# The softmax probabilities of a step kept in two tiles, one for each exp

## The chip, the core and the metric

The kernel runs on one core of one Trainium2 chip. A core has engines that run their own instruction streams in parallel and meet through semaphores: TensorE (PE: matmuls; its weight loads are shown as PEld), VectorE (DVE), ScalarE (ACT), GpSimd (POOL) and SyncE (SP, which here issues most DMAs). Matmul results land in PSUM, everything else on the chip lies in SBUF, and big tensors lie in DRAM.

The metric is the time of one execution on the device in microseconds (us); the median over several runs is compared.

## The reference, cut to what matters

A transformer block on 2048 tokens of width 448 with 16 heads of 28, modulated by a vector `c`:

```
mod = silu(c) @ w_mod                       # sa, ca, ga, sb, cb, gb
h = layernorm(x) * (1 + ca) + sa
q, k, v = split_heads(h @ wqkv)             # 16 heads of 28
p = softmax(q k^T / sqrt(28))
x = x + ga * ((p v) @ wo)
h = layernorm(x) * (1 + cb) + sb
x = x + gb * (gelu(layernorm(h) @ w1 + b1) @ w2 + b2)
```

The change lies in the attention: `p` and its product with `v`.

## The kernel before, in words

**Stages.** A first phase makes the modulation, the layer norm, Q, K and V, and some of the row maxima of the scores. The attention follows, and then the MLP. Float32 values are split into a high and a low part in several places, so that products are made as hi*hi + lo*hi + hi*lo.

**The attention loop** (`for u in range(NU)`, line 1140). A unit `u` is a group of four heads and a block of 512 queries: 4 x 4 = 16 units. A unit has 16 steps `kt`, one for each block of 128 keys, so there are 256 steps. A step does, in this order of issue:

- line 1152: takes the tile `pt` for the probabilities of the step: 128 keys x 4 heads x 512 queries.
- lines 1158 to 1168, for the two halves `hf` (heads 0 and 1, then heads 2 and 3): six scores matmuls into a PSUM tile of two banks (line 1163: three terms for each of two heads, the first with 29 rows, of which the last brings in the row maximum, the others with 28), and then one exp by ScalarE over the two banks into the half of `pt` (line 1168). Between them stand matmuls for row maxima of later units (`emit_max`, matmul line 466), each followed by a reduction on VectorE (line 471) that frees its PSUM tile. A step has three or four of them in turn while there are any left.
- line 1174: the product of probabilities and V of the step *before* (`av`, line 1133), so that TensorE has something to do while ScalarE makes the exps.
- tasks due in this step (line 1182): the end of earlier units, loads, in the last four units the output projection (`t_wo`), and in the end the preparation of the MLP.

Two PSUM tiles for scores (`s1`, `s0`) go in turn, so that the first half of a step waits for the first exp of the step before, and the second half for its second exp. When all maxima are done, a third one is opened (`third_tile`). Three PSUM tiles serve the maxima in this loop.

**What sets the order.** The program is written out in the order in which each engine issues it; no scheduler moves instructions. The tile layer only adds the waits: an instruction that reads or overwrites a tile waits for the semaphores of those that wrote or read it before. It knows the parts of a tile: of a tile `[128, 4, 512]` the two halves are kept apart when read, while a new tile in the same slot waits for all that used the old one. An instruction holds one wait; where it needs more, the others stand on event-semaphore instructions ahead of it in the same engine's stream.

**The slots.** `slot(tag, ...)` (line 77) gives a piece of SBUF by name, used by one tile after another. `c0`, `c1` and `d0` are 4 x 512 float32 on each partition, and are used through the whole kernel: for the modulation weights (`wm_ac`, line 164), the parts of `h` of odd token blocks (`hT`, line 283), as scratch for a Relu (`pair_diff`, line 477), for the probabilities (`ptags`, line 1138, in turn by `step % 3`), and in the end for parts of `w1` and `w2` (lines 1008 to 1094). `slot4` (line 83) hands out a four-part slot, for the tags in `halved` as two tiles with names `tag` and `tag + "h"`.

Of the kernel before, what the change touches and what calls it, by code (L numbers as in the profile page):

```python
# [13 lines left out]
F32 = mybir.dt.float32  # L14
F32R = mybir.dt.float32r
AF = mybir.ActivationFunctionType
# [6 lines left out]
D = 448  # L23
# [3 lines left out]
NC = 4  # L27
# [8 lines left out]
SCALE = float(DH) ** -0.5  # L36
# [3 lines left out]
def tile_adaln_block(ctx: ExitStack, tc: tile.TileContext, x, wqkv, wo, w1, b1, w2, b2, c, w_mod, out):  # L40
    nc = tc.nc
    pe, act, dve, pool, sp = nc.tensor, nc.scalar, nc.vector, nc.gpsimd, nc.sync
# [27 lines left out]
    def nm(t):  # L70
        uid[0] += 1
        return f"{t}_{uid[0]}"
# [4 lines left out]
    def slot(tag, shape, dt=F32R):  # L77
        return sb.tile(shape, dt, tag="slot_" + tag, name=nm("slot_" + tag), bufs=1)


    halved = ("a2", "a3", "b1")

    def slot4(tag, inner):
        if tag not in halved:
            t = slot(tag, [128, 4] + inner)
            return lambda k: t[:, k]
        t2 = [slot(tag + h, [128, 2] + inner) for h in ("", "h")]
        return lambda k: t2[k // 2][:, k % 2]

    def ps_s2():  # L90
# [4 lines left out]
    def ps_s():  # L95
        return ps_tile("pa", 2)
# [11 lines left out]
    def f(t):  # L108
        return t.bitcast(F32)
# [11 lines left out]
    sa_col, ca_col = cols[:, 0:NC], cols[:, NC:]  # L121


    d0 = slot("d0", [128, 4, 512], F32)
    sil_b = d0[:, 0, 0 : NC * 32].rearrange("p (k r) -> p k r", r=32)
    c_rows = d0[0:NC, 1, :128]
    sp.dma_start(c_rows[0:3], c[0, 0:384].rearrange("(k p) -> k p", p=128))
    acc = [sbt(f"acc{b}", [128, 4, D]) for b in range(NB)]

# [13 lines left out]
    def load_w(cs, dst):  # L143
        for k in range(3):
            sp.dma_start(dst(k), wqkv[128 * k : 128 * k + 128, cs])
        sp.dma_start(dst(3)[0:64], wqkv[384:D, cs])
        sp.dma_start(dst(3)[64:128], wqkv[384:D, cs])

    def load_mod(dst, k, c0, n):
        if k < 3:  # L150
            sp.dma_start(dst[:, : n * D], w_mod[128 * k : 128 * k + 128, c0 : c0 + n * D])
        else:
            for h in range(2):
                x0 = c0 + h * n * D // 2
                sp.dma_start(dst[64 * h : 64 * h + 64, : n * D // 2], w_mod[384:D, x0 : x0 + n * D // 2])


    def mod_part(k, j, n):
        if k < 3:
            return slice(0, 128), slice(j * D, (j + 1) * D)  # L160
        h, j = divmod(j, n // 2)
        return slice(64 * h, 64 * h + 64), slice(j * D, (j + 1) * D)

    wm_ac = [slot(f"c{i}", [128, 2, 2 * D], F32) for i in range(2)]
    for k in range(NC):
        load_mod(wm_ac[k // 2][:, k % 2, :], k, 0, 2)
    load_w(slice(0, 2 * D), lambda k: raw_qk[k // 2][:, k % 2, :])
    sp.dma_start(acc[1], xv[1])
    load_w(slice(2 * D, 3 * D), lambda k: raw_v[:, k, :])
# [126 lines left out]
    pm = ps_s()  # L296
# [11 lines left out]
    for k in range(NC):  # L308
        for j in range(2):
            rs_, cs = mod_part(k, j, 2)  # L310
            pe.matmul(
                pm[32 * j : 32 * j + 32, :D], sil_b[rs_, k, :], wm_ac[k // 2][rs_, k % 2, cs],
                start=(k == 0), stop=(k == NC - 1),
            )
    warm_up(2)
# [18 lines left out]
    v_sb = [sb.tile([128, 4, H, 32], F32, tag=f"slot_v{i}", name=f"v{i}", bufs=1) for i in range(4)]  # L334
# [15 lines left out]
    def by_head(t):  # L350
        return t.rearrange("(j r) n -> j r n", r=32)

    ones = d0[0:4, 0, 128:384]
    pool.memset(ones, 1.0)

    ones_d = dr.tile([4, S], F32, tag="ones", name="ones_d", bufs=1)
# [100 lines left out]
    px_no = [0]  # L457

    def max_mm(g, qt, i, j, k, ps=None):
        if (g, qt) not in mxp:  # L460
            mxp[(g, qt)] = sbt("mxp", [128, 4, 4, 4], bufs=6)
            if (g, qt) in paired:
                pool.memset(mxp[(g, qt)][:, :, :, 0:1], -3.0e38)
        m = (ps or ps_mx)()
        js = slice(32 * j, 32 * j + DH)
        pe.matmul(m, qh_sb[(g, qt)][js, i * 128 : (i + 1) * 128], k[js, :], start=True, stop=True)  # L466
        return m
# [6 lines left out]

    def pair_diff(g, qt, i, j):
        m = max_mm(g, qt, i, j, k_diff[0])
        r = d0[:, 1 + px_no[0] % 3]
        px_no[0] += 1
        act.activation(r, m, AF.Relu)  # L479

        def rest(ps):
            m = max_mm(g, qt, i, j, kh_sb[(g, 0)], ps)
            dve.tensor_tensor_reduce(
                out=r, in0=m, in1=r, scale=1.0, scalar=-3.0e38, op0=ALU.add, op1=ALU.max,
                accum_out=mxp[(g, qt)][:, i, j, 1:2],
            )

        return rest
# [121 lines left out]
    def finish_max(g, qt):  # L610
        while left[(g, qt)] > 0:
            emit_max(1)
# [47 lines left out]
    def load_q(u):  # L660
        g, qt = divmod(u, NB)
        qst[u] = load_parts(f"b{u % 2}", 0, g, slice(qt * 512, (qt + 1) * 512))
# [21 lines left out]
    for n, i in (  # L684
# [7 lines left out]
        p, ts = firsts[n]  # L692
# [3 lines left out]
    for b in range(NB):  # L696
# [12 lines left out]
        for n, (tb, kind, g) in enumerate(tasks):  # L709
# [9 lines left out]
            k = n - (6, 4, 4, 4)[b]  # L719
# [17 lines left out]
            if more:  # L737
                k = n - (6, 4, 4, 4)[b]
# [266 lines left out]
    w1t = {}  # L1005
    w2t = {}

    def w1_item(q, k, tags):
        n = 512 if q < 3 else 256
        fs = slice(512 * q, 512 * q + n)  # L1010

        def ld(r):
            if k < 3:
                sp.dma_start(r[:, :n], w1[128 * k : 128 * k + 128, fs])
            else:
                sp.dma_start(r[0:64, :n], w1[384:D, fs])
                sp.dma_start(r[64:128, :n], w1[384:D, fs])

        def go(r):
            if q not in w1t:  # L1020
                if q < 3:
                    w1t[q] = [slot4(tags[part], [512]) for part in range(2)]
                else:
                    t = slot(tags[0], [128, 2, NC, 256])
                    w1t[q] = [lambda k: t[:, 0, k], lambda k: t[:, 1, k]]
            hi, lo = w1t[q][0](k), w1t[q][1](k)
            w_copy[0](hi, r[:, :n])
            dve.tensor_tensor(out=lo, in0=r[:, :n], in1=f(hi), op=ALU.subtract)

        return ld, go  # L1030
# [56 lines left out]
    items = [w1_item(0, k, (q0, "a0")) for k in range(NC)]  # L1087
# [2 lines left out]
    items += [w2_item(ft, ("v2", "v3")) for ft in range(4, 8)]  # L1090
    items += [w1_item(2, k, ("a3", "c0")) for k in range(NC)]
    items += [w2_item(ft, ("d0", q1)) for ft in range(8, 12)]
    items += [w1_item(3, k, ("c1",)) for k in range(NC)]
    items += [w2_item(ft, ("e0",)) for ft in range(12, NFT)]
    w_prep = Prep(items)
    at(last0 + 2, lambda: w_prep.load(2))
# [11 lines left out]
    o = None  # L1108
# [21 lines left out]
    def av(u, kt, p, o):  # L1130
        g = u // NB
        for j in range(4):
            pe.matmul(  # L1133
                o[32 * j : 32 * j + 32, :], v_sb[kt // 4][:, kt % 4, 4 * g + j, :], p[:, j, :],
                start=(kt == 0), stop=(kt == NKT - 1),
            )

    ptags = ["d0", "c0", "c1"]
    done_max = set()
    for u in range(NU):  # L1140
        g, qt = divmod(u, NB)
        for kt in range(NKT):
            step = u * NKT + kt
            if kt == 1 and u + 1 < NU and u + 1 not in qst:
                load_q(u + 1)
            if kt == NKT - 6 and u + 1 < NU:
                finish_max(*divmod(u + 1, NB))
            tick_late()
            if not (three or mxq or late):
                three = True  # L1150
                third_tile(True)
            pt = slot(ptags[step % 3], [128, 4, 512], F32)
            n = n_maxima(step)
            n0 = 1 if n == 3 and step % 4 == 3 else 2

            ks, qs = kst[(g, kt // 4)], qst[u]
            kc = slice((kt % 4) * 128, (kt % 4 + 1) * 128)
            for hf in range(2):
                s2 = ps_s2()
                for term, (kp, qp) in enumerate(((0, 0), (1, 0), (0, 1))):  # L1160
                    for jj in range(2):
                        rows_ = slice(64 * hf + 32 * jj, 64 * hf + 32 * jj + DH + (term == 0))
                        pe.matmul(s2[:, jj, :], ks[rows_, kp, kc], qs[rows_, qp, :], start=(term == 0), stop=(term == 2))  # L1163
                    if hf == 0 and term < min(n0, n):
                        emit_max(1, 1)
                    if hf == 1 and term == 2 and n > n0:
                        emit_max(n - n0, 0)
                act.activation(pt[:, 2 * hf : 2 * hf + 2, :], s2, AF.Exp, scale=SCALE)  # L1168
            if step == 0:
                v_task(NB - 1, 3, ps_mx())  # L1170
                emit_max(2)
            if pend is not None:
                pu, pkt, pp, po = pend
                av(pu, pkt, pp, po)
                if pkt == NKT - 1:
                    end_unit(pu, po)
            if kt == 0:
                o = ps_o()
            pend = (u, kt, pt, o)
            if qt == NB - 1 and kt % 4 == 3 and g + 1 < NG:  # L1180
                load_k(g + 1, kt // 4 if g else kt // 4 ^ 2)
            for fn in sched.pop(step, ()):
                fn()
# [58 lines left out]
    for n in range(len(seq) + LAG):  # L1242
        if n < len(seq):
            b, i = seq[n]
# [53 lines left out]
```

## Time and profile before

| what | us |
|---|---|
| median of 3 runs | 1136.1 |
| lowest, highest | 1134.84, 1137.12 |
| span of the profiled execution | 1133.1 |
| attention loop, first to last exp | 169.4 to 838.0 |
| ScalarE busy in the whole span | 671.4 |
| of it exps of line 1168 (512) | 329.6 + 166.8 |
| VectorE busy in the whole span | 843.6 |
| of it maxima of line 471 into `mxp` from `m` (884) | 568.8 |

The span runs from the first to the last instruction of one execution recorded by the profiler; the runs' times also hold what lies around it. Lines of the profile name an engine, a source line, an operation, and what it writes and reads ("slot_c<-s": into a slot c0 or c1 from a score tile), with numbers of buffers left out. PE rows can overlap each other, since matmuls are pipelined and those on different rows or columns of the array run side by side. A "q" behind an engine's name means its sequencer.

### The profile page before, as it was taken

The numbers are of one execution on the slowest core, as the hardware profiler recorded it, in microseconds if no ns is written. First come the engines' busy times: TensorE is split into PE (matmuls) and PEld (weight loads), VectorE is DVE, ScalarE is ACT, GpSimd is POOL, SyncE is SP. The second block draws the span as 40 slices with busy tenths as digits, with TensorE's granted clock in tenths as the row PEclk, the third lists the DMA queues.
The fourth block names the chain that finished last, engine by engine and source line by source line (L and its number), as shares of the span: only waits on it lengthen the run. The fifth ranks groups of instructions, "written<-read, shape, count | busy, mean of one in ns | idle before, by whom it ended". The sixth has DMA issues, their size and how long they took to land.

```text
span 1133.1 us, 20660 instructions
## 1 busy us (share of the span) xinstructions
PE 1123.2 (99%) x8319; PEld 673.8 (59%) x8319; DVE 843.6 (74%) x1485; ACT 671.4 (59%) x823; POOL 209.8 (19%) x211
## 2 busy tenths in 40 slices
PE   9999999999999999999999999999999999999998
PEld 6756674444444444444444454545468888888887
DVE  6868788999999999999999978595348853444322
ACT  4555667777777877787787867576862321211110
POOL 2533332010000000000000010207114503123000
PEclk9999999999999999999999999999999999999999
DMA  8562263121221211211111312020422100000000
GB/s 309 203 206 77 86 213 100 46 85 39 68 84 57 58 39 57 86 57 58 48 48 57 104 49 76 11 85 1 136 57 86 43 33 1 1 33 1 33 1 33
DMA packets 49341, 81.19 MB, mean 72 GB/s; under 512 B 12311, under 2 KB 18702, under 8 KB 49234
## 3 DMA queue, kind: packets, MB, share of 16 engines
q1 hardware_dynamic: 48762, 79.14, 22.2%
q8 instruction: 65, 1.06, 0.4%
q10 hardware_dynamic: 148, 0.46, 0.1%
q0 software_dynamic: 336, 0.28, 0.1%
q14 instruction: 30, 0.25, 0.1%
HBM read 55.04 MB, written 26.48 MB: 72 GB/s over the span
## 4 chain that ended last, share of the span: by engine, by line
PE 93%; DVE 3%; DMA 1%; ACT 1%; issue 1%; SPq 0%; DVEq 0%; POOL 0%; POOLq 0%; ACTq 0%
PE s L1163 27%; PE o L1133 22%; PE m L386 16%; PE pa L386 8%; PE m L466 6%; PE s L1233 3%; PE s L1232 3%; PE s L1234 3%; DVE mxp L471 2%; PE t L1233 1%; PE t L1234 1%; PE t L1232 1%; PE o L267 1%; PE ma L466 1%; DMA slot_c<-in_w_mod_dram 1%
## 5 line engine op out<-in xcount | busy, mean ns | idle before, releaser
L471 DVE TENSOR_REDUCE mxp<-m 128x1 f32<-128x512 f32 x884 | 568.8, 685 | 81.4 <-PE m L466 44.6
L1163 PE MATMUL s<-slot_b,slot_a 28*128 28x512 f32 (+1 forms) x3072 | 383.3, 422 | 0.3
L1168 ACT ACTIVATE slot_c<-s 128x1024 f32<-128x1024 f32 x340 | 329.6, 1022 | 82.4 <-PE s L1163 82.2
L1163 PEld LDWEIGHTS s<-slot_b,slot_a 28*128 28x128 f32 (+1 forms) x3072 | 216.4, 184 | 251.3 <-ACT slot_c L1168 149.4
L466 PE MATMUL m<-kh,qh 28*128 28x512 f32 x863 | 286.0, 472 | 0.9 <-DVE mxp L471 0.5
L1168 ACT ACTIVATE slot_d<-s 128x1024 f32<-128x1024 f32 x172 | 166.8, 1022 | 42.1 <-PE s L1163 42.0
L1133 PE MATMUL o<-slot_c,v 128*32 128x512 f32 x1360 | 181.2, 605 | 0.0
L1209 ACT ACTIVATE full<-m,b_col 128x512 f32<-128x512 f32 x56 | 38.6, 688 | 191.9 <-PE m L386 179.7
L1212 DVE CAST hi<-full 128x512 fp32r<-128x512 f32 x56 | 25.2, 450 | 135.2 <-ACT full L1209 135.2
L466 PEld LDWEIGHTS m<-kh,qh 28*128 28x128 f32 x863 | 114.3, 182 | 6.6 <-DVE mxp L471 4.7
L895 POOL TENSOR_TENSOR osb<-osb,osb 128x512 f32<-128x512 f32 x16 | 20.9, 1308 | 448.3 <-DMA osb<-drec 306.9
L1133 PE MATMUL o<-slot_d,v 128*32 128x512 f32 x688 | 92.5, 605 | 0.6 <-ACT osb L1102 0.4
L386 PE MATMUL m<-y,slot_a 128*128 128x512 f32 x160 | 60.7, 395 | 0.0
L1133 PEld LDWEIGHTS o<-slot_c,v 128*32 128x32 f32 x1360 | 26.8, 108 | 53.5 <-issue 52.8
L1213 DVE TENSOR_TENSOR lo<-full,hi 128x512 fp32r<-128x512 f32 x56 | 44.1, 788 | 5.9 <-DVE hi L1212 0.9
L386 PE MATMUL m<-y,slot_c 128*128 128x512 f32 x152 | 47.5, 396 | 0.1
L471 DVE TENSOR_REDUCE mxp<-ma 128x1 f32<-128x512 f32 x54 | 35.6, 682 | 7.2 <-PE m L466 4.1
L386 PE MATMUL m<-y,slot_v 128*128 128x512 f32 x112 | 39.2, 396 | 0.0
L386 PE MATMUL m<-y,slot_b 128*128 128x512 f32 x112 | 39.0, 397 | 0.0
L479 ACT ACTIVATE slot_d<-m 128x512 f32<-128x512 f32 x33 | 18.8, 597 | 31.5 <-PE m L466 18.0
L1234 PE MATMUL s<-slot_v,lo 128*128 128x448 f32 x96 | 35.0, 365 | 0.0
L1232 PE MATMUL s<-slot_v,hi 128*128 128x448 f32 x96 | 35.0, 364 | 0.0
(272 smaller groups left out, 1434.0 us busy)
## 6 DMA issues: line engine op xcount, KB each, us to landing
slot_b<-d SPq DMA_DIRECT2D x32, 256.0 KB
slot_a<-d SPq DMA_DIRECT2D x32, 256.0 KB
d<-lo SPq DMA_DIRECT2D x28, 256.0 KB
d<-hi SPq DMA_DIRECT2D x16, 256.0 KB
osb<-drec SPq DMA_DIRECT2D x15, 256.0 KB
out_dram<-xn SPq DMA_DIRECT2D x16, 224.0 KB
raw<-in_B_w_dram SPq DMA_DIRECT2D x14, 224.0 KB
qh<-d SPq DMA_DIRECT2D x12, 256.0 KB
```

Source lines behind the costliest of these rows:

```text
L386: pe.matmul(p, a, b, start=(i == 0), stop=(i == len(terms) - 1))
L466: pe.matmul(m, qh_sb[(g, qt)][js, i * 128 : (i + 1) * 128], k[js, :], start=True, stop=True)
L471: dve.tensor_reduce(out=mxp[(g, qt)][:, i, j, cch : cch + 1], in_=m, op=ALU.max, axis=AX.X)
L1133: pe.matmul(o[32 * j : 32 * j + 32, :], v_sb[kt // 4][:, kt % 4, 4 * g + j, :], p[:, j, :], start=(kt == 0), stop=(kt == NKT - 1),)
L1163: pe.matmul(s2[:, jj, :], ks[rows_, kp, kc], qs[rows_, qp, :], start=(term == 0), stop=(term == 2))
L1168: act.activation(pt[:, 2 * hf : 2 * hf + 2, :], s2, AF.Exp, scale=SCALE)
L1209: act.activation(gf, p, AF.Gelu_apprx_tanh, bias=b1_col[:, i : i + 1])
L1212: dve.tensor_copy(ghi, gf)
L1213: dve.tensor_tensor(out=glo, in0=gf, in1=f(ghi), op=ALU.subtract)
L1232: pe.matmul(pp, ghi[:, ts], w_hi, start=(m == 0), stop=False)
L1233: pe.matmul(pp, ghi[:, ts], w_lo, start=False, stop=False)
L1234: pe.matmul(pp, glo[:, ts], w_hi, start=False, stop=(m == NFT - 1))
```

## The change

The tile of probabilities of a step becomes two tiles of two heads each, one written by each exp. The first half takes the slots `d0`, `c0`, `c1` in turn (a step uses the same slot as three steps before), the second half `c0h` and `c1h` in turn (the same as two steps before). To have these names, `c0`, `c1` and `d0` join `halved`, and all other users of these slots get two tiles where they had one. The slot `d0h` is used by the Relu scratch and by `w2` only.

```diff
-    halved = ("a2", "a3", "b1")
+    halved = ("a2", "a3", "b1", "c0", "c1", "d0")
 
-    def slot4(tag, inner):
+    def slot4(tag, inner, dt=F32R):
         if tag not in halved:
-            t = slot(tag, [128, 4] + inner)
+            t = slot(tag, [128, 4] + inner, dt)
             return lambda k: t[:, k]
-        t2 = [slot(tag + h, [128, 2] + inner) for h in ("", "h")]
+        t2 = [slot(tag + h, [128, 2] + inner, dt) for h in ("", "h")]
         return lambda k: t2[k // 2][:, k % 2]
...
-    d0 = slot("d0", [128, 4, 512], F32)
-    sil_b = d0[:, 0, 0 : NC * 32].rearrange("p (k r) -> p k r", r=32)
-    c_rows = d0[0:NC, 1, :128]
+    d0 = slot4("d0", [512], F32)
+    sil_b = d0(0)[:, 0 : NC * 32].rearrange("p (k r) -> p k r", r=32)
+    c_rows = d0(1)[0:NC, :128]
...
-    wm_ac = [slot(f"c{i}", [128, 2, 2 * D], F32) for i in range(2)]
+    wm_ac = [slot(f"c{i}{h}", [128, 2 * D], F32) for i in range(2) for h in ("", "h")]
     for k in range(NC):
-        load_mod(wm_ac[k // 2][:, k % 2, :], k, 0, 2)
+        load_mod(wm_ac[k], k, 0, 2)
...
-                pm[32 * j : 32 * j + 32, :D], sil_b[rs_, k, :], wm_ac[k // 2][rs_, k % 2, cs],
+                pm[32 * j : 32 * j + 32, :D], sil_b[rs_, k, :], wm_ac[k][rs_, cs],
...
-    ones = d0[0:4, 0, 128:384]
+    ones = d0(0)[0:4, 128:384]
...
-        r = d0[:, 1 + px_no[0] % 3]
+        r = d0(1 + px_no[0] % 3)
...
-                    t = slot(tags[0], [128, 2, NC, 256])
-                    w1t[q] = [lambda k: t[:, 0, k], lambda k: t[:, 1, k]]
+                    w1t[q] = [lambda k, t=slot(tag, [128, NC, 256]): t[:, k] for tag in tags]
...
-    items += [w1_item(3, k, ("c1",)) for k in range(NC)]
+    items += [w1_item(3, k, ("c1", "c1h")) for k in range(NC)]
...
-                o[32 * j : 32 * j + 32, :], v_sb[kt // 4][:, kt % 4, 4 * g + j, :], p[:, j, :],
+                o[32 * j : 32 * j + 32, :], v_sb[kt // 4][:, kt % 4, 4 * g + j, :], p[j // 2][:, j % 2, :],
...
-    ptags = ["d0", "c0", "c1"]
+    ptags = (["d0", "c0", "c1"], ["c0h", "c1h"])
...
-            pt = slot(ptags[step % 3], [128, 4, 512], F32)
+            pt = [slot(tags[step % len(tags)], [128, 2, 512], F32) for tags in ptags]
...
-                act.activation(pt[:, 2 * hf : 2 * hf + 2, :], s2, AF.Exp, scale=SCALE)
+                act.activation(pt[hf], s2, AF.Exp, scale=SCALE)
```

## The prediction

> **What bounds the kernel now.** I read the page first: busy times, the chain that ended last, the costliest groups.
>
> ```profile
> span 1133.1 us, 20660 instructions
> PE 1123.2 (99%) x8319; PEld 673.8 (59%) x8319; DVE 843.6 (74%) x1485; ACT 671.4 (59%) x823; POOL 209.8 (19%) x211
> PE 93%; DVE 3%; DMA 1%; ACT 1%; issue 1%; SPq 0%; DVEq 0%; POOL 0%; POOLq 0%; ACTq 0%
> L1163 PE MATMUL s<-slot_b,slot_a 28*128 28x512 f32 (+1 forms) x3072 | 383.3, 422 | 0.3
> ```
>
> By this TensorE is everything and ScalarE nothing. But these matmuls overlap each other, so that a late start of one hides under the end of another: 3072 of 422 ns would be 1296 us in sequence, and they are busy for 383. So I read the waits next, where the weight loads stand for the start of a matmul:
>
> ```profile
> PEld s L1163 <- ACT slot_c L1168: 149.4, 222, 1.1
> ACT slot_c L1168 <- PE s L1163: 82.2, 164, 1.2
> PEld s L1163 <- ACT slot_d L1168: 74.2, 111, 0.9
> ACT slot_d L1168 <- PE s L1163: 42.0, 83, 1.6
> ```
>
> The scores matmuls wait for the exps (333 times) and the exps for the scores (164 + 83 = 247 times in 256 steps). Two engines that wait for each other are a loop, so the timeline of two steps comes third (start, length, engine, line):
>
> ```profile
> 501.90 1.94 ACT L1168 ACTIVATE slot_c<-s 128x1024 f32<-128x1024 f32 x2 [0.80 <-PE s L1163]
> 503.03 0.50 PE L1163 MATMUL s<-slot_b,slot_a 29*128 29x512 f32 x2
> 503.37 0.63 PE L1163 MATMUL s<-slot_b,slot_a 28*128 28x512 f32 x4
> 503.89 0.49 PE L1163 MATMUL s<-slot_b,slot_a 29*128 29x512 f32 x2
> 504.09 1.94 ACT L1168 ACTIVATE slot_c<-s 128x1024 f32<-128x1024 f32 x2 [0.26 <-PE s L1163]
> 504.45 0.40 PE L1163 MATMUL s<-slot_b,slot_a 28*128 28x512 f32 x2
> 504.78 1.07 PE L1133 MATMUL o<-slot_c,v 128*32 128x512 f32 x8
> 505.78 0.50 PE L1163 MATMUL s<-slot_b,slot_a 29*128 29x512 f32 x2
> 506.84 1.94 ACT L1168 ACTIVATE slot_d<-s 128x1024 f32<-128x1024 f32 x2 [0.81 <-PE s L1163]
> ```
>
> The pair of exps from 501.90 ends at 503.84 and frees the second score tile; the next step's second half of scores starts 0.05 later, at 503.89, though its first half had started at 503.03. From there to the PV matmuls at 504.78 are 0.89; these issue for 1.00, to the scores of the step after at 505.78; and 1.06 later, at 506.84, the exps of that step start. 1.94 + 0.05 + 0.89 + 1.00 + 1.06 = 4.94 us, which is 506.84 − 501.90: a closed loop over two steps. The steps between form the same loop, shifted (504.09 + 1.94 = 506.03, and so on). Each loop crosses once per two steps the way from the last matmul of a first half to its exp. That way is what the change touches.
>
> **The change part by part.** As built, every engine has the same instructions in the same order before and after: no DMA, copy or matmul is added or moved. What differs is which waits each exp carries. An instruction waits for one semaphore itself; a second one is put on a separate event-semaphore instruction ahead of it.
>
> ```profile
> L1168 ACTq EVENT_SEMAPHORE  x254: 17/17/828, 168.5 to 836.0; - x127
> 501.17 0.63 PE L1163 MATMUL s<-slot_b,slot_a 28*128 28x512 f32 x6
> 176.48 0.64 PE L1163 MATMUL s<-slot_b,slot_a 28*128 28x512 f32 x6
> 177.16 1.03 ACT L1168 ACTIVATE slot_c<-s 128x1024 f32<-128x1024 f32 x1 [0.61 <-PE s L1163]
> 174.04 0.50 PE L1163 MATMUL s<-slot_b,slot_a 28*128 28x512 f32 x3
> 174.60 1.03 ACT L1168 ACTIVATE slot_c<-s 128x1024 f32<-128x1024 f32 x1 [1.21 <-PE s L1163]
> ```
>
> *First exp of a step.* Before, it opens a tile whose last writer was the second exp three steps ago, so it carries that wait beside the one for its scores, and the wait for the scores stands on the separate instruction. After, the tile's last writer is a first exp, which the order of semaphores already covers: one wait, no separate instruction. Its price: with it the exp starts 504.09 − (503.37 + 0.63) = 0.09 and 501.90 − (501.17 + 0.63) = 0.10 after the last matmul ends. Steps 1 and 2, the first users of c0 and c1, have none: 177.16 − (176.48 + 0.64) = 0.04, 174.60 − (174.04 + 0.50) = 0.06. Between 0.03 and 0.06 saved; I take 0.055, nearer the row of an undisturbed step.
>
> [...]
>
> *Second exp of a step.* It takes over the separate instruction: its tile, on two slots in turn, was last written by the second exp two steps ago. What hides it is the first exp, which runs meanwhile: in the four-maxima step the second half's last scores end at 504.45 + 0.40 = 504.85, and the second exp starts at 504.09 + 1.94 − 1.02 = 505.01, 0.16 later, where a wait with the extra instruction needs 0.10. Both ends move with the loop, so 0.06 stays. That the instruction passes while the engine works is shown once, in step 0, the only one whose second exp has it already:
>
> ```profile
> 169.39 1.94 ACT L1168 ACTIVATE slot_d<-s 128x1024 f32<-128x1024 f32 x2 [0.36 <-PE s L1163]
> L1168 ACTq EVENT_SEMAPHORE  x1: 17/17/17, 170.1 to 170.1; - x1
> 504.09 1.03 ACT L1168 ACTIVATE slot_c<-s 128x1024 f32<-128x1024 f32 x1 [0.26 <-PE s L1163]
> ```
>
> It stands at 170.1, inside the exp from 169.39, and the pair is still done in 1.94. If this cover were gone, the pair would lose its overlap (one exp 1.03, two 1.94: 0.10) and the 0.055 besides.
>
> *Slots.* The second half on two slots instead of three waits for nothing new: the PV matmuls that read the tile two steps ago stand ahead of this step's scores in TensorE's order, and the exp waits for the scores anyway. For the same reason the first half's third slot gains nothing. Both: 0.
>
> *How many loops.* Busy time by stretch (window, its length, then PE, PEld, DVE, ACT, POOL):
>
> ```profile
> 410.00:449.60 39.60, 39.60 (x379) 17.93 (x378) 36.69 (x61) 31.52 (x33) 2.57 (x2) 1.00 0.13 41
> 694.80:744.90 50.10, 49.73 (x425) 26.34 (x424) 35.19 (x59) 33.65 (x38) 7.18 (x7) 1.00 0.16 49
> 792.80:838.00 45.20, 44.61 (x376) 21.86 (x372) 18.79 (x30) 35.29 (x41) 7.70 (x6) 1.00 0.39 114
> ```
>
> A unit of 16 steps takes 39.6 (2.475 a step, half the loop). That holds for units 0 to 11; in units 12 to 14 (second row) four of 16 steps also hold the output projection, 12 matmuls each, and are longer than the loop; in unit 15 (third row) the maxima are gone, VectorE falls to 18.79, and with a third score tile I count nothing. 192 − 2 + 12 + 12 + 8 = 222 steps, 111 loops. 111 × 0.055 = 6.1 us off.
>
> *Step 0.* Here the halves cost something: the second exp of step 0 now lies in c0h, which the last V matmuls, issued after it, still read.
>
> ```profile
> 172.04 0.78 PE L386 MATMUL m<-slot_e,slot_c 128*128 128x448 f32 x3
> 172.86 0.53 ACT L448 COPY v<-m 128x448 f32<-128x448 f32 x1 [1.54 <-PE m L386]
> 174.03 0.49 PE L466 MATMUL m<-kh,qh 28*128 28x512 f32 x1
> ```
>
> It starts at about 172.82 + 0.10 = 172.92 instead of 170.31; the copy of V, behind it on ScalarE, ends at 172.92 + 0.92 + 0.53 + 0.05 = 174.42 instead of 173.39. The second maximum of step 1 reuses the V result's tile and as built now waits for that copy: 174.42 instead of 174.03, with the rest of step 1's scores behind it. +0.4 us, once.
>
> *The other edits* (modulation weights in four tiles, the Relu scratch, the last w1 quarter and hi/lo h in halves) change waits of five POOL instructions in the first phase, POOL being 19% busy, and none of DVE, SP or the tail: 0.
>
> **Sum:** −6.1 + 0.4 = −5.7. From the profiled execution's 1133.1 span this makes 1127.4; the median of the runs stands 3.0 above that span, so 1136.1 − 5.7 = 1130.4.
>
> **The rivals.** *VectorE takes the gain over.* The fourth maximum of a step reuses the tile of the first:
>
> ```profile
> 503.61 0.69 DVE L471 TENSOR_REDUCE mxp<-m 128x1 f32<-128x512 f32 x1 [0.15 <-PE m L466]
> 504.35 0.50 PE L466 MATMUL m<-kh,qh 28*128 28x512 f32 x1
> 503.21 0.24 DVE L886 RECIPROCAL den<-den 128x16 f32<-128x16 f32 x1
> 516.02 0.42 DVE L905 CAST hi<-osb 128x512 fp32r<-128x512 f32 x1
> ```
>
> It starts at 504.35, 0.05 after that reduce ends, and its rows are free 0.33 later (as 503.03 to 503.37), 0.10 ahead of the PV matmuls at 504.78. After the change 0.045 is left, still positive, which is why this isn't the forecast. But in each of some 14 units VectorE has other work (a reciprocal, a cast, a transpose, a reduce of maxima), and where one falls ahead of the first reduce the loop's gain is lost there: 14 × 4 × 0.055 = 3.1, leaving 1133.5. Against it: VectorE is busy 36.69 of 39.60, so it recovers.
>
> *TensorE is the bound after all:* the page's 99% and a chain with ACT at 1% speak for it, the closed sum of 4.94 against. Then the change doesn't do what its waits say: 1136.1 + 0.4 = 1136.5. [...]
>
> *Slower:* the separate instruction ahead of the second exp drains ScalarE, in every step of the loop. Each loop then loses 0.10 + 0.055 and gains 0.055: 111 × 0.10 = 11.1, +0.4, 1147.6. It decides from 0.055 of lost overlap on. For it: step 0 is one case. Against: that case. [...]
>
> **How the numbers follow.** Forecast 0.66, with its own range 1128.8 to 1133.2 (0.03 and 0.06 saved are 3.3 and 6.7 us, less 0.4: 1133.2 and 1129.8; below it 1 us, about what the three runs of before, 1134.84 to 1137.12, stand off their median); VectorE 0.15; TensorE 0.12; slower 0.07. The range from 1128.0 to 1134.8 leaves out the last two, 0.19. About 0.2%, 2.3 us, is what can be told from no change: faster holds the forecast and most of the VectorE case, 0.80; same 0.13; slower 0.07.
>
> **What would show it.** Right: the event-semaphores of the exp's line stand inside a running exp; first exps start 0.04 after their last scores instead of 0.09 to 0.10; a unit takes 39.2 (16 × 2.475 − 8 × 0.055); step 0 to step 1 is longer by 0.4; pairs of exps still last 1.94. Wrong: pairs of 2.05 or more (slower); the 0.04 present but units at 39.6, with the fourth maximum right ahead of the PV matmuls (VectorE), or these no earlier after their scores (TensorE).

## The result, and the profile after

| what | before | after |
|---|---|---|
| median of the runs, us | 1136.1 (1134.84 to 1137.12) | 1128.9 (1128.23 to 1130.08) |
| ratio | | 0.994, 95% interval 0.9928 to 0.9952 |
| span of the profiled execution, us | 1133.1 | 1128.0 |

The change makes the kernel 7.2 us faster; the interval of the ratio, on 1136.1, reaches from 5.5 to 8.2 us. The page of the kernel after, the same rows as before (the last gives busy time and mean duration in ns):

```profile
span 1128.0 us, 20665 instructions
PE 1116.4 (99%) x8319; PEld 670.1 (59%) x8319; DVE 843.7 (75%) x1485; ACT 672.0 (60%) x823; POOL 209.6 (19%) x211
PE 94%; DVE 3%; ACT 1%; DMA 1%; issue 1%; POOL 0%; SPq 0%; DVEq 0%; ACTq 0%; POOLq 0%
L1162 PE MATMUL s<-slot_b,slot_a 28*128 28x512 f32 (+1 forms) x3072 | 376.3, 420 | 0.0
```

Nothing here tells where the time went. Every engine does the same work (8319 matmuls, ScalarE 671.4 and 672.0 us busy; the 5 instructions more are event-semaphores), and TensorE is "99%" busy as before, though the program is shorter. The same scores matmuls are busy for 376.3 us instead of 383.3. Since the profile models the ends of matmuls, I read these 7 us as waiting that had been booked as busy; no run shows it directly. The waits say more (engine and tile that waited, what ended it, then the sum in us, how often, the longest):

```profile
PEld s L1162 <- ACT slot_c L1167: 124.1, 148, 0.8
ACT slot_c L1167 <- PE s L1162: 75.6, 163, 0.8
PEld s L1162 <- ACT slot_d L1167: 62.1, 74, 0.8
ACT slot_d L1167 <- PE s L1162: 39.1, 81, 1.7
PEld s L1162 <- ACT slot_c1h L1167: 34.4, 110, 0.3
```

ScalarE's wait for the scores fell from 82.2 + 42.0 to 75.6 + 39.1, by 9.5 us, at almost the same number of waits (247 and 244); 2.4 us of it come back as a wait in step 0, shown below. TensorE still waits for the exps. (By name the rows on its side are split otherwise, since the second exps now have slots of their own.) Here is the loop of two steps, as in the prediction, at another place of the same kind:

```profile
499.06 1.02 ACT L1167 ACTIVATE slot_c<-s 128x1024 f32<-128x1024 f32 x1 [0.81 <-PE s L1162]
499.98 1.02 ACT L1167 ACTIVATE slot_c1h<-s 128x1024 f32<-128x1024 f32 x1
500.19 0.50 PE L1162 MATMUL s<-slot_b,slot_a 29*128 29x512 f32 x2
500.52 0.64 PE L1162 MATMUL s<-slot_b,slot_a 28*128 28x512 f32 x4
501.05 0.18 PEld L1162 LDWEIGHTS s<-slot_b,slot_a 29*128 29x128 f32 x2 [0.33 <-ACT slot_c1h L1167]
501.20 1.03 ACT L1167 ACTIVATE slot_c<-s 128x1024 f32<-128x1024 f32 x1 [0.20 <-PE s L1162]
501.51 0.49 PE L466 MATMUL m<-kh,qh 28*128 28x512 f32 x1
501.62 0.39 PE L1162 MATMUL s<-slot_b,slot_a 28*128 28x512 f32 x2
501.94 0.62 PE L1132 MATMUL o<-slot_c,v 128*32 128x512 f32 x2
502.12 1.02 ACT L1167 ACTIVATE slot_c0h<-s 128x1024 f32<-128x1024 f32 x1
502.94 0.49 PE L1162 MATMUL s<-slot_b,slot_a 29*128 29x512 f32 x2
503.93 1.02 ACT L1167 ACTIVATE slot_d<-s 128x1024 f32<-128x1024 f32 x1 [0.79 <-PE s L1162]
```

The pair of exps takes 499.98 + 1.02 − 499.06 = 1.94; 0.05 later, at 501.05, the second half's scores start; 0.89 to the PV matmuls at 501.94, 1.00 to the next step's scores at 502.94, 0.99 to its exp at 503.93. The sum is 4.87 against 4.94. Only the last term, from the scores to their exp, differs: 0.99 for 1.06. The first half's last scores end at 500.52 + 0.64 = 501.16 and the exp starts at 501.20, 0.04 later; before it was 0.09 to 0.10. Over all first exps that waited, the median distance from the end of the last scores is 39 ns (before: 100).

What moved is the separate event-semaphore instruction. In the kernel before it stands right ahead of the first exp (the exp at 504.09 in the prediction's timeline):

```profile
L1168 ACTq EVENT_SEMAPHORE  x1: 17/17/17, 504.0 to 504.0; - x1
```

In the kernel after there is about one for each step too (257 for 254), but ahead of the second exp, and in the stretch from 500.90 to 502.13 the only one is at 502.1, just ahead of the exp of 502.12:

```profile
L1167 ACTq EVENT_SEMAPHORE  x257: 17/17/828, 169.3 to 831.1; - x129
L1167 ACTq EVENT_SEMAPHORE  x1: 17/17/17, 502.1 to 502.1; - x1
```

Now the whole program. First exps of the units 1, 12 and 15, before and then after:

```profile
211.80 1.03 ACT L1168 ACTIVATE slot_c<-s 128x1024 f32<-128x1024 f32 x1 [0.24 <-PE s L1163]
647.84 1.02 ACT L1168 ACTIVATE slot_d<-s 128x1024 f32<-128x1024 f32 x1 [0.28 <-PE s L1163]
792.81 1.02 ACT L1168 ACTIVATE slot_d<-s 128x1024 f32<-128x1024 f32 x1 [0.18 <-PE s L1163]
```

```profile
212.59 1.03 ACT L1167 ACTIVATE slot_c<-s 128x1024 f32<-128x1024 f32 x1 [0.22 <-PE s L1162]
643.07 1.03 ACT L1167 ACTIVATE slot_d<-s 128x1024 f32<-128x1024 f32 x1 [0.23 <-PE s L1162]
787.14 1.02 ACT L1167 ACTIVATE slot_d<-s 128x1024 f32<-128x1024 f32 x1
```

Units 1 to 11 took 436.04 and take 430.48: 5.56 less, 0.51 a unit. Units 12 to 14 took 144.97 and take 144.07: 0.90 less. Together 6.5. The profiled spans differ by less, 5.1, because in this one execution of the kernel after the first exp came at 170.26 instead of 169.39 and unit 15 took 45.69 instead of 45.23, 1.3 us in all. A second profile of the same kernel (the run *e7_change_again* below) has the first exp at 169.41, unit 15 in 44.89 and a span of 1126.0, so these 1.3 us are scatter and no effect of the change.

### The profile page after: what moved, and what is told of

It is laid out like the page before. It is cut to its first block, busy times and chain, and to the rows that moved or that the text cites. A ratio compares the mean times of both kernels' runs of the same rounds, so it can differ in the third digit from the quotient of the medians.

```text
span 1128.0 us, 20665 instructions
## 1 busy us (share of the span) xinstructions
PE 1116.4 (99%) x8319; PEld 670.1 (59%) x8319; DVE 843.7 (75%) x1485; ACT 672.0 (60%) x823; POOL 209.6 (19%) x211
## 3 DMA queue, kind: packets, MB, share of 16 engines
q8 instruction: 65, 1.06, 0.4%
## 4 chain that ended last, share of the span: by engine, by line
PE 94%; DVE 3%; ACT 1%; DMA 1%; issue 1%; POOL 0%; SPq 0%; DVEq 0%; ACTq 0%; POOLq 0%
PE s L1162 26%; PE o L1132 22%; PE m L386 16%; PE pa L386 8%; PE m L466 6%; PE s L1232 3%; PE s L1233 3%; PE s L1231 3%; DVE mxp L471 2%; PE t L1232 1%; PE t L1233 1%; PE t L1231 1%; DMA slot_c<-in_w_mod_dram 1%; PE ma L466 1%; PE o L267 1%
## 5 line engine op out<-in xcount | busy, mean ns | idle before, releaser
L1162 PE MATMUL s<-slot_b,slot_a 28*128 28x512 f32 (+1 forms) x3072 | 376.3, 420 | 0.0
L1162 PEld LDWEIGHTS s<-slot_b,slot_a 28*128 28x128 f32 (+1 forms) x3072 | 213.0, 184 | 247.4 <-ACT slot_c L1167 124.1
L1167 ACT ACTIVATE slot_c<-s 128x1024 f32<-128x1024 f32 x170 | 174.3, 1025 | 75.9 <-PE s L1162 75.6
L1132 PE MATMUL o<-slot_c,v 128*32 128x512 f32 x680 | 178.8, 605 | 0.0
L1132 PE MATMUL o<-slot_c1h,v 128*32 128x512 f32 x512 | 134.7, 605 | 0.0
L1132 PE MATMUL o<-slot_c0h,v 128*32 128x512 f32 x512 | 134.7, 605 | 0.0
L1167 ACT ACTIVATE slot_c0h<-s 128x1024 f32<-128x1024 f32 x128 | 130.4, 1019 | 2.4 <-PE m L386 2.4
L1167 ACT ACTIVATE slot_c1h<-s 128x1024 f32<-128x1024 f32 x128 | 130.4, 1019 | 0.0
L1167 ACT ACTIVATE slot_d<-s 128x1024 f32<-128x1024 f32 x86 | 88.1, 1025 | 39.3 <-PE s L1162 39.1
L1132 PEld LDWEIGHTS o<-slot_c,v 128*32 128x32 f32 x680 | 24.5, 108 | 52.4 <-issue 49.5
```

Source lines behind the costliest of these rows:

```text
L1132: pe.matmul(o[32 * j : 32 * j + 32, :], v_sb[kt // 4][:, kt % 4, 4 * g + j, :], p[j // 2][:, j % 2, :], start=(kt == 0), stop=(kt == NKT - 1),
L1167: act.activation(pt[hf], s2, AF.Exp, scale=SCALE)
```

## The experiments

The theory: the gain is the time from the last scores to the first exp, shorter because the wait for the scores no longer stands on a separate instruction; it comes back once in each closed loop of two steps. Rivals: the gain is the finer tiles as such, or the number of slots, or an easier start.

**Two tiles, three slots for each half** (beside the change):

```diff
-    ptags = (["d0", "c0", "c1"], ["c0h", "c1h"])
+    ptags = (["d0", "c0", "c1"], ["d0h", "c0h", "c1h"])
```

> Halves in two tiles as in the change, but both on three slots (d0h added to the second half). As built, both exps of a step then carry a second wait, so the wait for the scores stands on a separate event-semaphore ahead of both. Theory W (the place of that instruction decides: 0.055 to 0.06 us a loop, 111 loops): first exps again 0.09 to 0.10 after their scores, a unit at 39.6, the time of the kernel before, 1135 to 1137. Theory H (two tiles, freed half by half, make the gain): 1128 to 1130, units at 39.1, since there are more slots than in the change.

As built, both exps of a step now carry a wait for the old writer of their slot beside the one for the scores. The instructions of the exp's line:

```profile
L1167 ACTq EVENT_SEMAPHORE  x504: 17/17/828, 169.0 to 836.7; - x168
```

Measured: 1136.57 against 1135.58 of the kernel before on the same chip, ratio 1.0009 (0.9999 to 1.0018). All of the gain is gone, though the tiles are split. First exps start 98 ns after their scores (median), and a unit takes 39.63 (median of units 1 to 11), 39.61 before. (Unit 5 follows. The row of a stretch: start:end, its length, then busy time of PE, PEld, DVE, ACT, POOL.)

```profile
371.21:410.82 39.61, 39.61 (x377) 17.74 (x376) 36.64 (x61) 31.52 (x33) 2.62 (x3) 1.00 0.18 55
```

**The change mirrored: the first half on two slots, the second on three.**

```diff
-    ptags = (["d0", "c0", "c1"], ["c0h", "c1h"])
+    ptags = (["c0", "c1"], ["d0h", "c0h", "c1h"])
```

> The mirror image of the change: first half on two slots (c0, c1), second half on three (d0h, c0h, c1h). As built the separate event-semaphore then stands ahead of the first exp alone, as before the change. Theory W: 1135 to 1137, units at 39.6. Theory H (halves), and also a theory that five half slots instead of three whole ones matter: 1128 to 1130.

Measured: 1135.36, ratio 0.9997 (0.9988 to 1.0007). The event-semaphores stand ahead of the first exps, their starts are 99 ns after the scores (median), and the gain is gone, with tiles of the same size and as many slots as in the change. In the change and in its mirror image the half with fewer slots carries the second wait; with three slots each, both halves do. Its instructions, and step 0 in the timeline:

```profile
L1167 ACTq EVENT_SEMAPHORE  x256: 17/17/820, 172.8 to 836.8; - x128
```

```profile
172.86 1.03 ACT L1167 ACTIVATE slot_c<-s 128x1024 f32<-128x1024 f32 x1 [2.45 <-PE m L386]
```

The first exp of all goes into `c0` and waits for the last V matmuls (line 386), which still read it: 172.86 instead of 169.39. The steps after it catch up most of that; unit 1 starts at 213.20, 1.4 later than before. The time doesn't show these 1.4. In the seven profiles in which the first exp doesn't wait for these matmuls it stands between 169.39 and 170.49, so that a start read from one profile is good to about 1 us.

**The kernel before, whole tiles, two slots instead of three.**

```diff
-    ptags = ["d0", "c0", "c1"]
+    ptags = ["c0", "c1"]
...
-            pt = slot(ptags[step % 3], [128, 4, 512], F32)
+            pt = slot(ptags[step % 2], [128, 4, 512], F32)
```

> The kernel before with its whole tiles on two slots (c0, c1) instead of three. The separate event-semaphore stays ahead of the first exp. My working puts the third slot at 0: 1135 to 1137, units at 39.6. A theory that slots coming free set the pace expects it slower by more than 1 us.

Measured: 1138.57, ratio 1.0026 (1.0016 to 1.0035). The expectation missed, and step 0 is why. Here too the first exp of all opens a slot that the V matmuls read, and what that costs is more than the expectation had:

```profile
174.59 1.94 ACT L1168 ACTIVATE slot_c<-s 128x1024 f32<-128x1024 f32 x2 [3.87 <-PE m L386]
```

The first exp comes 5.2 late; unit 0 makes up 2.14 of it (40.27 for 42.41), and unit 1 starts 3.06 later than before, close to the 3.0 that the times show. The loop itself is untouched: the median of units 1 to 11 is 39.60, before 39.61. So the third slot is worth nothing in the loop, for whole tiles as for halves, and something at the start.

**The change with step 0's second exp in `d0h`,** so that it doesn't wait for the V matmuls:

```diff
-    ptags = (["d0", "c0", "c1"], ["c0h", "c1h"])
+    ptags = (["d0", "c0", "c1"], ["d0h", "c0h"])
```

> The change with the second half on d0h and c0h instead of c0h and c1h, so that step 0 writes d0h, which the last V matmuls don't read. Waits of all later steps as in the change. Theory W with my price for step 0 (0.4 us predicted, 0.32 in the profile of the change): 1128.6, the first step back from 5.54 to 5.2, units at 39.1. If the longer first step had another cause, it stays at 5.5.

Step 0 in the change, and then here:

```profile
170.26 1.03 ACT L1167 ACTIVATE slot_d<-s 128x1024 f32<-128x1024 f32 x1 [0.41 <-PE s L1162]
173.72 1.02 ACT L1167 ACTIVATE slot_c0h<-s 128x1024 f32<-128x1024 f32 x1 [2.44 <-PE m L386]
175.80 1.02 ACT L1167 ACTIVATE slot_c<-s 128x1024 f32<-128x1024 f32 x1 [0.63 <-PE s L1162]
```

```profile
170.49 1.03 ACT L1167 ACTIVATE slot_d<-s 128x1024 f32<-128x1024 f32 x1 [0.42 <-PE s L1162]
171.41 1.02 ACT L1167 ACTIVATE slot_d0h<-s 128x1024 f32<-128x1024 f32 x1
175.63 1.03 ACT L1167 ACTIVATE slot_c<-s 128x1024 f32<-128x1024 f32 x1 [1.22 <-PE s L1162]
```

In the change the second exp idles 2.44 us for the V matmuls, and step 1 comes 5.54 after step 0; with `d0h` it runs right behind the first, and step 1 comes 5.14 after. The 0.4 is step 0's whole price. In time it can't be told from the change: 1128.71, ratio 0.9939 (0.9924 to 0.9954).

**The separate instruction put back ahead of the first exp, in the kernel after.** A column of zeros is written two steps ahead by another engine and read by the first exp as its bias, which gives it a second wait and leaves the result as it is. POOL and VectorE take the part of the writer:

```diff
+    zt = slot("d0h", [128, 2, 512], F32)
+    zb = lambda k: zt[:, 0, k % 8 : k % 8 + 1]
+    pool.memset(zt[:, 0, 0:8], 0.0)
...
+            pool.memset(zb(step + 2), 0.0)
...
-                act.activation(pt[hf], s2, AF.Exp, scale=SCALE)
+                act.activation(pt[hf], s2, AF.Exp, scale=SCALE, **({} if hf else {"bias": zb(step)}))
```

Beside the engine that writes, the two differ as built in one thing: with POOL the wait for the scores goes to the separate instruction and the exp itself holds the early wait; with VectorE (`dve.memset` in the same places) it is the other way round.

> The change, with the first exp's bias read from a column of zeros that POOL writes two steps ahead, so that the first exp waits for POOL beside the scores. As built the wait for the scores goes to a separate event-semaphore and the long done wait for POOL to the exp. Theory W: first exps 0.09 to 0.10 after their scores again, units at 39.6, 1135 to 1137, though tiles and slots are those of the change. Theory H: as the change, 1128 to 1130.

> The same with VectorE writing the zeros. As built the separate event-semaphore then holds the long done wait for VectorE, and the exp itself the wait for the scores. Theory W in the form that the late wait must stand on the exp itself: the separate instruction is there but is over early, first exps 0.04 after their scores, 1128 to 1131 (some 250 small writes more on VectorE may cost a little). Theory W in the form that any separate instruction ahead of the first exp costs 0.06: 1135 to 1137.

Measured on one chip, where the kernel before took 1136.0: POOL 1145.53, ratio 1.009 (1.0075 to 1.0105); VectorE 1139.43, ratio 1.0035 (1.0021 to 1.005). Both are above what I expected, by a cost that I had left out: the exps that read a bias from SBUF took 1115 ns here instead of 1024. The instructions of the exp's line (ns, shortest/median/longest; then, for the event-semaphores of a short stretch, when they stood), first of the kernel after, then with POOL, then with VectorE:

```profile
L1167 ACT ACTIVATE slot_c<-s x170: 1024/1024/1054, 175.8 to 829.0; 128x1024 f32<-128x1024 f32 x170
```

```profile
L1171 ACT ACTIVATE slot_c<-s,slot_d0h x170: 1114/1115/1138, 175.6 to 844.7; 128x1024 f32<-128x1024 f32 x170
...
L1171 ACTq EVENT_SEMAPHORE  x1: 17/17/17, 500.7 to 500.7; - x1
```

```profile
L1171 ACT ACTIVATE slot_c<-s,slot_d0h x170: 1114/1115/1138, 175.7 to 838.2; 128x1024 f32<-128x1024 f32 x170
...
L1171 ACTq EVENT_SEMAPHORE  x2: 17/17/17, 500.2 to 500.3; - x2
```

The timeline around them, with POOL and with VectorE: the first half's last scores and the first exp, with VectorE also the second exp of the step before.

```profile
500.05 0.62 PE L1166 MATMUL s<-slot_b,slot_a 28*128 28x512 f32 x4
...
500.77 1.12 ACT L1171 ACTIVATE slot_c<-s,slot_d0h 128x1024 f32<-128x1024 f32 x1 [0.25 <-PE s L1166]
```

```profile
500.89 1.02 ACT L1171 ACTIVATE slot_c1h<-s 128x1024 f32<-128x1024 f32 x1
...
501.43 0.64 PE L1166 MATMUL s<-slot_b,slot_a 28*128 28x512 f32 x4
...
502.10 1.12 ACT L1171 ACTIVATE slot_d<-s,slot_d0h 128x1024 f32<-128x1024 f32 x1 [0.20 <-PE s L1166]
```

And the same unit, with POOL and with VectorE:

```profile
374.79:415.07 40.28, 40.28 (x379) 18.22 (x378) 36.74 (x61) 32.94 (x34) 3.69 (x19) 1.00 0.18 54
```

```profile
372.50:412.31 39.81, 39.81 (x379) 17.89 (x381) 36.87 (x77) 32.95 (x34) 2.63 (x3) 1.00 0.18 55
```

Three readings:

- *Late or early wait.* With POOL the instruction stands at 500.7, after the scores, which end at 500.05 + 0.62 = 500.67, and the exp starts at 500.77, 0.10 after them. With VectorE the two event-semaphores at 500.2 and 500.3 belong to the second exp of that step and to the first of the next, at 502.10: the latter has passed 1.8 us ahead, and the exp starts 502.10 − 502.07 = 0.03 after its scores. The medians are 99 and 38 ns; the change, with no separate instruction there, has 39. Tiles, slots, exps and their durations are the same, and a unit takes 40.28 and 39.81: 0.47, or 0.059 for each of its 8 loops. The times differ by 6.1 us, and 111 loops of 0.059 are 6.5. This is the change's effect, taken away and given back by where one wait stands; POOL's memsets are not what the exps wait for: they run two steps ahead, and ScalarE's idle time before the exp of 500.77 ends with the scores (0.25 <-PE s).
- *What the early instruction costs.* Nothing that can be seen: 38 ns with it, 39 without. It passes at 500.3, while the exp ahead of it in the program, the second one of that step, has yet to start, at 500.89. So an event-semaphore passed here 0.6 us before an exp that stands ahead of it had started.
- *The loop.* VectorE's version against the change: the exp is 1115 − 1024 = 91 ns longer, a unit 39.81 − 39.13 = 0.68, 0.085 a loop. So 0.09 us put into the pair of exps comes back nearly whole in each loop; 111 times 0.09 are 10.1, and 1128.4 + 10.1 = 1138.5 is near the 1139.4 measured.

**The change again,** on the chip of the last two:

> The changed kernel once more, for a second profile: units at 39.1 again in every theory. The first phase (first exp at 170.3 instead of 169.4 us) and the last unit (0.46 longer) were longer in its first profile, where the waits hardly differ: if that is scatter of one execution, they come back near 169.4 and 45.2; if the change causes it, they stay.

Measured: 1128.43, ratio 0.9939 (0.9925 to 0.9954). Its units 1 to 11 take 39.13 again (median) and step 0 takes 5.53. Unit 15 takes 44.89, and the first exp is where before had it (169.39), so the longer first phase and last unit were scatter:

```profile
169.41 1.03 ACT L1167 ACTIVATE slot_d<-s 128x1024 f32<-128x1024 f32 x1 [0.42 <-PE s L1162]
```

## Why the prediction was right, point by point

- *What bounds the kernel.* Right: the loop of exps, scores and PV matmuls, not TensorE by itself. A shorter way from scores to exp (the change) and a longer exp (the version with VectorE) both come back about once a loop, and the 99% of TensorE moved with neither.
- *First exp.* Right in its place, a little small in size: 0.055 taken, between the ends 0.03 and 0.06. Units fell from 39.61 to 39.13 (median of units 1 to 11), 0.48 over 8 loops, 0.060. That the old writer is "already covered" was put too simply: it is covered because the second half has *two* slots. Its second exp, one step ago, waited for the one three steps ago, which lies behind the first exp of that step; with three slots it waits for an older one, and the cover is gone (the first experiment). A unit of the kernel after, against the 39.60 of the prediction:

```profile
369.13:408.26 39.13, 39.13 (x379) 17.47 (x381) 36.68 (x61) 31.61 (x34) 2.62 (x3) 1.00 0.19 56
```

- *Second exp.* Right that it costs nothing, wrong about the margin. I wrote that 0.16 lies between its last scores and its start, that 0.10 is needed, and that 0.06 stays since both ends move with the loop. In the four-maxima step above the scores end at 501.62 + 0.39 = 502.01 and the exp starts at 502.12, 0.11 later. The exp moved up by the 0.05 that its pair gained, and the scores did not: they start when the second exp of the step before ends. The pair still takes 1.94, but with only 0.01 left. An estimate from these numbers: another 0.02 off the first exp's start would leave ScalarE idle between the two.
- *How many loops.* Right: 111. Units 12 to 14, with 12, 12 and 8 steps in the loop, gained 0.34, 0.32 and 0.24; 6, 6 and 4 loops of 0.060 are 0.36, 0.36 and 0.24.
- *Step 0.* Right: +0.4 predicted. The step is 0.32 longer than before (5.54 for 5.22) and 0.4 longer than with `d0h`. *Slots:* right, 0 in the loop; the working left out the start, and the version with two whole slots shows 3 us there.
- *VectorE.* Its slack was said to shrink from 0.10 to 0.045. It didn't: from a first half's scores to the PV matmuls the kernel before has 504.78 − 503.03 = 1.75, the kernel after 501.94 − 500.19 = 1.75, and from the fourth maximum to the PV matmuls both have 0.43 (504.78 − 504.35, 501.94 − 501.51). That stretch runs from exp to exp and through TensorE's issue, and the change does not touch it. What became shorter is the step with three maxima, 501.20 − 499.06 = 2.14 for 504.09 − 501.90 = 2.19; the one with four is 2.73 for 2.75. The loop fixes the sum of two steps, not how they share it, and I had put the gain into the wrong one. So the place at which this rival was to decide came no nearer, and no unit lost its gain there: units 1 to 11 take 39.11 to 39.16.
- *Slower.* Ruled out by the pair of 1.94, and by the three slots for each half: there the second exp has a separate instruction too, and the time is that of before.
- *The sum.* −5.7 predicted, 7.2 measured, 1130.4 and 1128.9. With the sizes measured, 111 × 0.060 − 0.4 = 6.3. Another 0.4 the prediction doesn't have: units 3 and 8 took 39.8 before where the others took 39.6, and after they don't. The rest, 0.5, is less than the runs scatter. The measured time lies just inside the forecast's own range, which began at 1128.8, and without these two terms it would have been near 1129.8.
- *Units 3 and 8.* Each holds one first exp that starts late after its event-semaphore, in unit 3 this one (in the first row, when the event-semaphore stood):

```profile
L1168 ACTq EVENT_SEMAPHORE  x1: 17/17/17, 323.4 to 323.4; - x1
323.71 1.94 ACT L1168 ACTIVATE slot_c<-s 128x1024 f32<-128x1024 f32 x2 [1.08 <-PE s L1163]
```

The exp starts 0.32 after the event-semaphore has passed, where the first exps around it start 0.045 after theirs. The other five versions have such units too (two to five of the eleven), and each holds one exp that starts 0.32 to 0.34 after an event-semaphore. In ScalarE's instructions, counted through the trace from 0, these exps always have a number that is 63 above a multiple of 128 (447 and 703 in the kernel before). The three profiles with the change's waits have no such unit: there these numbers fall in units 1 to 11 on second exps whose event-semaphore passed some 0.6 us earlier, and on first exps that have none. By this, the 0.4 come from the same move of the instruction, but how much it is depends on where the count falls. No step of the prediction had it, so this part of the gain was luck. What happens at these instructions is not shown.

What binds after a further cut of the same kind was not tried: no version here has both exps free of the separate instruction.

## What to carry to other kernels

Where, as here, an instruction with two waits has one of them on a separate instruction ahead of it, see that this is the wait that ends early, by the choice of buffers or of the order in which they were last written: from the scores to the exp it was 99 ns with the late wait there (the version with POOL), 38 with the early one (VectorE). Here it was worth 0.06 us at each crossing and 0.6% of the program, with no work changed. Look for closed loops between two engines by following one period of the timeline: a duration in the loop counted nearly in full once a period here (0.085 of 0.091), whatever the busy shares said.

## What was not expected of the hardware

On ScalarE here a separate event-semaphore cost by which wait it held: 0.06 us where it held the one that ended last (99 ns from the scores to the exp, with POOL), nothing that can be seen where it held an early one (38 ns with VectorE, 39 with none in the change). And the exps of 128x1024 that read their bias from a column of zeros in SBUF took 1115 ns instead of 1024. And where such an instruction stood ahead of an exp whose number among ScalarE's instructions is 63 above a multiple of 128, the exp started 0.32 us after it instead of 0.045 in the kernel before (instructions 447 and 703).
